# Spreading one row of a weight load unevenly over the DMA engines, reordering the last sums, and narrowing an early product to two column groups

## The chip, the cores and the metric

The kernel runs on one core of a Trainium2 chip. The metric is the device time of one execution in microseconds (us), as the median of several runs. "Span" is the shorter stretch from the first to the last instruction that the profile shows; here the time is mostly 2.0 to 2.6 us longer than the span, and over 3 us longer in three runs. A single run scatters by about 0.2 us.

## The reference

It is one decoding step of a layer, for one token: attention over a cache of 65,536 keys plus a gated feed-forward branch, on the same normalized input.

```python
xn = layernorm(x)
q = (xn @ wq)                                   # 1024 -> 32 heads of 128
scores = q . k_cache * 128**-0.5                # 4 key heads, 65,536 keys of 128
A = softmax(scores) @ v_cache  @ wo             # 4096 -> 1024
# the w1/w2 part shifts tokens; with one token only the zero padding reaches w2, so it adds 0
B = xn + gelu(layernorm(xn) @ w3) @ w4          # 1024 -> 3584 -> 1024
out = x + A + B
```

All of it is one vector times large matrices. 169.87 MB have to be read once, and nothing is reused, so the kernel streams.

## The kernel before

Loads of up to 8 MB go into three large buffers in the order wq, w3, w1 and w2, then K and V eight times, wo before the last V, and w4 last. SyncE issues every one. w4 has 3,584 rows of 2 KB, 28 for each of 128 partitions, and comes in pieces, so that TensorE can follow the landing:

```python
W4_PIECES = (8, 12, 5, 2, 1)         # rows of each partition
...
w4_v = B_w4.rearrange("(m c) n -> m c n", c=FC)          # FC = 28
c0 = 0
for n in W4_PIECES:
    go(out=t[:, c0 * D:(c0 + n) * D], in_=w4_v[:, c0:c0 + n, :].rearrange("p c n -> p (c n)"))
    c0 += n
```

The early product with wq uses four column groups of TensorE (32 output columns each). Its 64 matmuls took 4.98 us, 78 ns each in the mean, while the profile puts 479 ns to one of them:

```python
row_matmul(psq, xn_rep, lambda c, i, a: wt[:, c, 16 * i:16 * (i + 1), a, :], (512, 512))
```

The end: rows of w4 are added to the attention's projection in `psB`; the last eight rows go in halves of 256 columns into `quarters`, where the earlier sums are injected in between.

```python
with tc.issue_after(projected):
    compute_w4(early, FC - NARROW)                          # 12 wide rows, second piece
nc.vector.tensor_tensor(out=sums[:], in0=psB[0:64, :], in1=tail["o"], op=ALU.add)
narrow_rows(FC - NARROW, FC - NARROW + AHEAD, start=True)   # 5 rows, third piece
for h in range(2):
    nc.tensor.matmul(quarters[h][...], lhsT=pick[...], rhs=sums[:, 256 * h:256 * (h + 1)], ...)
narrow_rows(FC - NARROW + AHEAD, FC)                        # 2 + 1 rows
# two copies to out_t, then the store
```

## Time and profile before

| | before |
|---|---|
| time, median of 3 runs | 401.01 us (400.86 to 401.06) |
| span of the profiled run | 398.6 us |
| share of the load queue | 98.9% of 16 engines' span |
| busy: TensorE, VectorE | 57%, 53% |
| last w4 row landed (packet records) | 396.02 us |
| last four matmuls begin | 396.48 us |

The page of the profile gives averages; the packet records of the trace give the end. They do not name the DMA engine of a packet, so the sixteen engines are followed as sixteen chains of packets, by the best fit of ends, starts and sizes; the order of sizes within an engine is known from the kernel, and the prediction below says how the records follow each other. What such a fit gives for certain is the list of sixteen ends; where two engines run within a few nanoseconds of each other, it can exchange them.

### The profile page before, as it was taken

The page shows a single profiled execution, that of the slowest core. Times are in us where ns is not written, and L with a number is a line of the kernel's source. Part 1 is how long each engine was busy: PE and PEld are TensorE (multiplying, and loading weights), DVE is VectorE, ACT ScalarE, POOL GpSimd, SP SyncE. Part 2 cuts the span into 40 slices and gives each one's busy share as a digit, 9 for nine tenths or more (in the row PEclk, how much of TensorE's full clock was granted, in tenths as well). Part 3 has the DMA queues.
Part 4 walks back from the last instruction along what each step waited for, and adds up shares of the span by engine and source line. Part 5 has one row for each costly group of instructions (what it writes and reads, how often), then busy time and mean ns, then how long its engine had stood idle before and what let it go on. Part 6 is the DMA issues. An engine that isn't in the chain of part 4 may idle for free.

```text
span 398.6 us, 2575 instructions
## 1 busy us (share of the span) xinstructions
PE 225.4 (57%) x1360; PEld 44.0 (11%) x866; DVE 210.7 (53%) x160; ACT 27.1 (7%) x35; POOL 5.8 (1%) x29
## 2 busy tenths in 40 slices
PE   0251960591569238733974296519462955394986
PEld 0210000010100010011001010200020101010132
DVE  0610010974296559633963795269439942894141
ACT  1001020003000200020002000200110001002000
POOL 2000000000000000000000000000000000000000
PEclk9995996596869787966695889679956896698799
DMA  9998999999999999999999999999999998999996
GB/s 421 421 443 376 446 427 480 454 421 421 416 428 427 421 467 449 427 421 427 423 441 421 447 454 434 416 427 421 441 436 427 447 447 383 416 462 424 413 432 257
DMA packets 4144, 170.03 MB, mean 427 GB/s; under 512 B 419, under 2 KB 421, under 8 KB 678
## 3 DMA queue, kind: packets, MB, share of 16 engines
q1 hardware_dynamic: 4128, 169.87, 98.9%
q8 instruction: 9, 0.15, 0.2%
q14 instruction: 1, 0.01, 0.0%
q10 hardware_dynamic: 6, 0.00, 0.0%
HBM read 169.87 MB, written 0.00 MB: 426 GB/s over the span
## 4 chain that ended last, share of the span: by engine, by line
DMA 56%; DVE 21%; PE 17%; ACT 2%; another core or an unknown queue 2%; issue 1%; SPq 0%; DVEq 0%; ACTq 0%
DMA big<-in_A_k_cache_dram 42%; DVE big L360 15%; PE sc L365 11%; DMA big<-in_B_w_dram 8%; DMA big<-in_A_wq_dram 6%; PE oacc L415 4%; DVE p_sb L386 2%; DVE mx L370 2%; ACT p_sb L383 2%; PE psq L290 1%; SPq L187 0%; PE pm_mx L372 0%; DVE m L374 0%; PE pm_mx L379 0%
## 5 line engine op out<-in xcount | busy, mean ns | idle before, releaser
L365 PE MATMUL sc<-big,qdiag 128*128 128x512 bf16 x512 | 129.6, 414 | 66.5 <-DVE big L360 61.0
L360 DVE STREAM_TRANSPOSE big<-big 128x4096 f32<-128x4096 f32 x32 | 139.4, 4413 | 50.1 <-DMA big<-in_A_k_cache_dram 50.1
L415 PE MATMUL oacc<-big,p_sb 128*32 128x512 bf16 x512 | 43.2, 504 | 34.5 <-DVE p_sb L386 34.5
L370 DVE TENSOR_REDUCE mx<-sc 128x1 f32<-128x2048 f32 x8 | 18.3, 2292 | 29.9 <-PE sc L365 29.9
L365 PEld LDWEIGHTS <-qdiag 128*128 128x128 bf16 x128 | 13.2, 103 | 178.3 <-issue 145.7
L383 ACT ACTIVATE p_sb<-sc,nball 128x2048 bf16<-128x2048 f32 x8 | 15.7, 1968 | 220.8 <-DVE nball L381 220.8
L386 DVE STREAM_TRANSPOSE p_sb<-p_sb 128x2048 bf16<-128x2048 bf16 x8 | 18.5, 2311 | 18.0 <-ACT p_sb L383 18.0
L415 PEld LDWEIGHTS <-p_sb 128*32 128x32 bf16 x512 | 16.2, 122 | 58.2 <-DVE p_sb L386 35.1
L290 PE MATMUL psh<-big,ln_rep_b 128*32 128x512 bf16 (+1 forms) x64 | 12.4, 942 | 8.9 <-DMA big<-in_B_w_dram 8.9
L455 PE MATMUL o_acc<-big,oT 128*1 128x512 bf16 x48 | 13.2, 447 | 2.4 <-ACT p_sb L383 2.4
L372 PE MATMUL pm_mx<-ident_f,mx 128*1 128x128 f32 x8 | 2.4, 296 | 19.1 <-DVE mx L370 19.1
L424 DVE SCALAR_TENSOR_TENSOR og<-oacc,wb,og 128x512 f32<-128x512 f32 x4 | 3.0, 751 | 18.5 <-PE oacc L415 18.5
L329 DVE STREAM_TRANSPOSE h_row<-h_row 128x896 bf16<-128x896 bf16 x1 | 1.1, 1111 | 22.0 <-ACT h_row L328 22.0
L241 PE MATMUL pm_ln<-ln_rowsum_a,ones_f 128*128 128x1 f32 x2 | 0.6, 348 | 12.8 <-DVE ln_rowsum_a L239 12.8
L437 PE MATMUL pm_e<-ol,sel8big 128*128 128x129 f32 x8 | 2.3, 370 | 9.7 <-DVE ol L436 9.7
L314 POOL COPY qdiag<-qx 32x32 bf16<-32x32 bf16 x16 | 3.3, 204 | 278.7 <-PE sc L365 250.7
L290 PE MATMUL psq<-big,ln_rep_a 128*32 128x512 bf16 x64 | 5.0, 479 | 3.7 <-DMA big<-in_A_wq_dram 3.7
L232 DVE STREAM_TRANSPOSE x_t<-x_row 32x256 bf16<-32x256 bf16 x4 | 2.5, 615 | 8.4 <-DMA x_row<-in_A_x_dram 8.3
L466 DVE TENSOR_TENSOR big<-o_acc,big 1x512 f32<-1x512 f32 x2 | 1.4, 679 | 10.3 <-PE o_acc L455 10.3
L227 PE MATMUL psB<-big,hT 128*32 128x512 bf16 x40 | 4.8, 380 | 1.4 <-DMA big<-in_B_w_dram 1.3
L302 DVE CAST q_row<-psq 128x512 bf16<-128x512 f32 x1 | 0.7, 692 | 7.6 <-PE psq L290 7.6
L379 PE MATMUL pm_mx<-ident_f,rep 1*128 1x1 f32 x8 | 1.8, 229 | 5.0 <-DVE rep L376 5.0
(100 smaller groups left out, 71.9 us busy)
## 6 DMA issues: line engine op xcount, KB each, us to landing
big<-in_A_wo_dram SPq DMA_DIRECT2D x1, 8192.0 KB, 35.7
big<-in_B_w_dram SPq DMA_DIRECT2D x1, 7168.0 KB, 38.1
big<-in_B_w_dram SPq DMA_DIRECT2D x3, 2048.0 KB, 35.5
big<-in_B_w_dram SPq DMA_DIRECT2D x1, 3072.0 KB, 29.5
big<-in_B_w_dram SPq DMA_DIRECT2D x1, 1280.0 KB, 32.2
big<-in_B_w_dram SPq DMA_DIRECT2D x1, 512.0 KB
big<-in_B_w_dram SPq DMA_DIRECT2D x1, 256.0 KB, 33.1
big<-in_A_k_cache_dram SPq DMA_DIRECT2D x8, 42.2
```

Source lines behind the costliest of these rows:

```text
L227: return nc.tensor.matmul(psB[32 * j:32 * j + 32, :], lhsT=lhsT.to_broadcast([lhsT.shape[0], 32]), rhs=rhs, start=start, stop=False, tile_ ...
L232: nc.vector.transpose(out=x_t[32 * a:32 * a + 32].rearrange("p c j -> p (c j)"), in_=x_row[:, 256 * a:256 * (a + 1)].rearrange("p (i c) -> ...
L290: nc.tensor.matmul(acc[32 * q:32 * q + 32, i, 0:n], lhsT=rep[:, c, :], rhs=cols(c, i, q), start=(c == 0), stop=(c == DC - 1), tile_positio ...
L314: nc.gpsimd.tensor_copy(out=qdiag[at, LEAD:].rearrange("p (x c) -> p x c", x=4)[:, :, 32 * a:32 * a + 8], in_=qx[at, :, 8 * g:8 * g + 8])
L360: nc.vector.transpose(out=words, in_=words)
L365: nc.tensor.matmul(sc[:, e, :], lhsT=qdiag[:, c0:c0 + P], rhs=cols[:, s, e, :, b2, :, r], start=(s == 0 and b2 == 0 and r == 0), stop=(s = ...
L370: nc.vector.reduce_max(out=mx[:], in_=sc[:].rearrange("p e n -> p (e n)"), axis=AX.X)
L383: nc.scalar.activation(out=p_sb[:], in_=sc[:], func=ACTF.Exp, bias=nball[:, b:b + 1], scale=SCALE, accum_out=group["lall"][:, b:b + 1])
L386: nc.vector.transpose(out=flat, in_=flat)
L415: mm = nc.tensor.matmul(oacc[32 * q:32 * (q + 1), :], lhsT=pT[:, e, 32 * t:32 * (t + 1)], rhs=vt[:, :, e, t, :], start=(e == 0 and t < 4), ...
L424: nc.vector.scalar_tensor_tensor(out=og[:], in0=oacc[:], scalar=wb[:, 1:2], in1=og[:], op0=ALU.mult, op1=ALU.add)
L455: nc.tensor.matmul(tail["rows"][0:1, h2, :], lhsT=oT[g][:, j:j + 1], rhs=wt[:, g, j, 512 * h2:512 * (h2 + 1)], start=(g == 0 and j == 0), ...
```

## The change

It takes row 27 (the 28th) of every partition out of the common load, and loads these 128 rows by seven small transfers on 3, 3, 3, 5, 8, 8 and 8 partitions, up to four rows to a partition. The intent, as the shares show it, is to use engines that finish early. GpSimd first zeroes the columns that take these rows. The four columns so filled need their h values at the same places; a 0/1 matrix, built at the start, puts them there by four small matmuls. What `tail["o"]` holds (x and the projection of the earlier heads) is injected ahead of the second piece; of the sums in `psB`, one half is injected ahead of the third piece, and the other is added in the last copy. Six rows of the first piece run before the gather of the last heads, in place of three (this edit of the diff is not printed below). wq runs on two column groups in place of four.

No record names an engine, so the numbers 0 to 15 in this document are labels for classes of chains: 0 to 2 carry packets of all seven small loads, 3 and 4 those of the loads on 5 and on 8 partitions, 5 to 7 those on 8 alone, 8 to 15 none. In the other runs a load on k partitions is likewise labelled as using 0 to k - 1. Which engines of the chip they are is not shown.

```diff
-W4_PIECES = (8, 12, 5, 2, 1)
+W4_PIECES = (8, 11, 5, 2, 1)
+LEFT = 4
+SHARES = ((3, 0, 4), (3, 1, 4), (3, 2, 4), (5, 3, 4), (8, 32, 4), (8, 33, 4), (8, 34, 1))
+WHOLE = 27
...
+                nc.gpsimd.memset(t[:, WHOLE * D:(WHOLE + LEFT + 1) * D].bitcast(F32), 0.0)
+                for share in SHARES[:3] + W4_PIECES[:1] + SHARES[3:] + W4_PIECES[1:]:
...
+                    k, i0, m = share
+                    go(out=t[i0:i0 + 4 * k:4, WHOLE * D:(WHOLE + m) * D].rearrange("e (i n) -> e i n", i=m),
+                       in_=w4_v[m0:m0 + k * m, WHOLE, :].rearrange("(i e) n -> e i n", e=k))
...
-        row_matmul(psq, xn_rep, lambda c, i, a: wt[:, c, 16 * i:16 * (i + 1), a, :], (512, 512))
+        row_matmul(psq, xn_rep, lambda c, i, q: wt[:, c, 16 * (i % 2):16 * (i % 2 + 1), q + 2 * (i // 2), :],
+                   (512, 512, 512, 512), groups=2)
...
+def place_left():                      # h of row 27 to the partitions that hold its rows
+    for x in range(LEFT):
+        nc.tensor.matmul(pm[:, x:x + 1], lhsT=place[:, x, :], rhs=h_left[:], start=True, stop=True)
...
+    with tc.issue_after(filled):
+        filled = compute_w4(WHOLE, WHOLE + LEFT)         # the four placed columns
...
     with tc.issue_after(projected):
-        compute_w4(early, FC - NARROW)
-    nc.vector.tensor_tensor(out=sums[:], in0=psB[0:64, :], in1=tail["o"], op=ALU.add)
+        for h in range(2):
+            begun = inject(h, pick[...], tail["o"][0:64, 256 * h:256 * (h + 1)], True)
+    with tc.issue_after(begun):
+        compute_w4(early, WHOLE - NARROW)
+    nc.scalar.copy(out=sums[0][:], in_=psB[0:64, 0:256])
+    nc.vector.tensor_copy(out=sums[1][:], in_=psB[0:64, 256:512])
...
+    with tc.issue_after(inject(0, ident_f[0:64, 0:64], sums[0][:], False)):
+        narrow_rows(WHOLE - NARROW, WHOLE)
```

More of the change, by code (lines that the diff above doesn't have):

```diff
@@ L20 @@
 SLOTS = 3
-W4_PIECES = (8, 12, 5, 2, 1)
-FIRST = 3
-AT_ONCE = 1
+W4_PIECES = (8, 11, 5, 2, 1)
+LEFT = 4
+SHARES = ((3, 0, 4), (3, 1, 4), (3, 2, 4), (5, 3, 4), (8, 32, 4), (8, 33, 4), (8, 34, 1))
+WHOLE = 27
+FIRST = 6
 NARROW = 8
-AHEAD = 5
 def keep_loaded_weights(nc):
@@ L126 @@
     assert DH == P and HQ // HKV == 8 and HKV == 4 and D == 1024 and F == 3584 and S == 1
-    assert SK % UKEYS == 0 and sum(W4_PIECES) == FC
+    assert SK % UKEYS == 0 and sum(W4_PIECES) == WHOLE == FC - 1
     NB = SK // UKEYS
@@ L184, in load @@
                 w4_v = B_w4.rearrange("(m c) n -> m c n", c=FC)
-                c0 = 0
-                for n in W4_PIECES:
-                    go(out=t[:, c0 * D:(c0 + n) * D], in_=w4_v[:, c0:c0 + n, :].rearrange("p c n -> p (c n)"))
-                    c0 += n
+                nc.gpsimd.memset(t[:, WHOLE * D:(WHOLE + LEFT + 1) * D].bitcast(F32), 0.0)
+                c0, m0 = 0, 0
+                for share in SHARES[:3] + W4_PIECES[:1] + SHARES[3:] + W4_PIECES[1:]:
+                    if share in W4_PIECES:
+                        go(out=t[:, c0 * D:(c0 + share) * D], in_=w4_v[:, c0:c0 + share, :].rearrange("p c n -> p (c n)"))
+                        c0 += share
+                        continue
+                    k, i0, m = share
+                    go(out=t[i0:i0 + 4 * k:4, WHOLE * D:(WHOLE + m) * D].rearrange("e (i n) -> e i n", i=m),
+                       in_=w4_v[m0:m0 + k * m, WHOLE, :].rearrange("(i e) n -> e i n", e=k))
+                    m0 += k * m
+                assert m0 == P and c0 == WHOLE
             else:
@@ L284, with row_matmul @@
         nc.vector.tensor_copy(out=x_halves[32 * j:32 * j + 1, :], in_=x_row[0:1, 512 * j:512 * (j + 1)])
-    def row_matmul(acc, rep, cols, widths):
+    place = ogpool.tile([P, LEFT, P], BF16, name="place", tag="og")
+    nc.gpsimd.memset(place[:], 0.0)
+    m0 = 0
+    for k, i0, m in SHARES:
+        cells = place[:, 0:m, i0:i0 + 4 * k:4].rearrange("p i e -> p e i")
+        nc.gpsimd.affine_select(out=cells, in_=cells, compare_op=ALU.not_equal, fill=1.0, base=-m0,
+                                pattern=[[-1, k], [-k, m]], channel_multiplier=1)
+        m0 += k * m
+    def row_matmul(acc, rep, cols, widths, groups=4):
         for c in range(DC):
             for i, n in enumerate(widths):
-                for q in range(4):
+                for q in range(groups):
                     nc.tensor.matmul(acc[32 * q:32 * q + 32, i, 0:n], lhsT=rep[:, c, :], rhs=cols(c, i, q),
@@ L298, in compute_wq @@
         psq = ps_S.tile([P, SUBS, 512], F32, name="psq", tag="sc")
-        row_matmul(psq, xn_rep, lambda c, i, a: wt[:, c, 16 * i:16 * (i + 1), a, :], (512, 512))
+        row_matmul(psq, xn_rep, lambda c, i, q: wt[:, c, 16 * (i % 2):16 * (i % 2 + 1), q + 2 * (i // 2), :],
+                   (512, 512, 512, 512), groups=2)
         st.done("wq")
         q_row = ppool.tile([P, 2, 512], BF16, name="q_row", tag="p")
-        nc.vector.tensor_copy(out=q_row[:, 0, :], in_=psq[:, 0, :])
-        nc.scalar.copy(out=q_row[:, 1, :], in_=psq[:, 1, :])
+        nc.vector.tensor_copy(out=q_row[0:64, :, :], in_=psq[0:64, 0:2, :])
+        nc.scalar.copy(out=q_row[64:128, :, :], in_=psq[0:64, 2:4, :])
         flat = q_row[:].rearrange("p i n -> p (i n)")
@@ L316, in place_queries @@
                 in_=qx[at, :, 8 * g:8 * g + 8])
-    hT = const.tile([P, FC], BF16, name="hT")
+    hT = const.tile([P, WHOLE + LEFT], BF16, name="hT")
+    h_left = const.tile([P, 1], BF16, name="h_left")
     def compute_w3():
@@ L329, in compute_w3 @@
         nc.vector.transpose(out=h_row[:], in_=h_row[:])
-        nc.vector.tensor_copy(out=hT[:], in_=h_row[:, ::32])
+        nc.vector.tensor_copy(out=hT[:, 0:WHOLE], in_=h_row[:, 0:32 * WHOLE:32])
+        nc.vector.tensor_copy(out=h_left[:], in_=h_row[:, 32 * WHOLE:32 * WHOLE + 1])
+    def place_left():
+        pm = ps_M.tile([P, 512], F32, name="pm_h", tag="pm")
+        for x in range(LEFT):
+            nc.tensor.matmul(pm[:, x:x + 1], lhsT=place[:, x, :], rhs=h_left[:],
+                             start=True, stop=True)
+        nc.vector.tensor_copy(out=hT[:, WHOLE:], in_=pm[:, 0:LEFT])
     def compute_w12():
@@ L403, with compute_v @@
     assert NB == 2
-    def compute_v(u):
+    def compute_v(u, fill=None):
         g, b = divmod(u, NB)
@@ L425, in compute_v, with group_rows @@
                                        op0=ALU.mult, op1=ALU.add)
-        group_rows(g, og, ol)
-        return mm.ins
+        group_rows(g, og, ol, fill and (lambda: fill(mm.ins)))
     oT = {}
     tail = {}
-    def group_rows(g, og, ol):
+    def group_rows(g, og, ol, fill):
         pe = ps_M.tile([P, 512], F32, name="pm_e", tag="pm")
@@ L436, in group_rows @@
         nc.vector.tensor_reduce(out=ol[:, 0:DH], in_=og[:].rearrange("p (s d) -> p d s", d=DH), axis=AX.X, op=ALU.add)
-        tail["gathered"] = nc.tensor.matmul(pe[:, 0:DH + 1], lhsT=sel8big[:], rhs=ol[:], start=True, stop=True).ins
+        if fill is None:
+            nc.tensor.matmul(pe[:, 0:DH + 1], lhsT=sel8big[:], rhs=ol[:], start=True, stop=True)
+        else:
+            with tc.issue_after(fill()):
+                tail["gathered"] = nc.tensor.matmul(pe[:, 0:DH + 1], lhsT=sel8big[:], rhs=ol[:], start=True, stop=True).ins
         msk = small.tile([P, 16, 8], F32, name="msk", tag="msk")
@@ L460, in copy_projection @@
     def copy_projection():
-        tail["o"] = st.tiles["w4"][0:64, FC * D:FC * D + D].bitcast(F32)
-        nc.vector.tensor_scalar(out=tail["o"], in0=x_halves[:], scalar1=ln_s1[0:64, 0:1], scalar2=ln_s2[0:64, 0:1],
+        tail["o"] = st.tiles["w4"][:, (WHOLE + LEFT) * D:(WHOLE + LEFT + 1) * D].bitcast(F32)
+        nc.vector.tensor_scalar(out=tail["o"][0:64, :], in0=x_halves[:], scalar1=ln_s1[0:64, 0:1], scalar2=ln_s2[0:64, 0:1],
                                 op0=ALU.mult, op1=ALU.add)
@@ L471, in compute_w4 @@
             for j in range(2):
-                row_acc(j, hT[:, c:c + 1], wt[:, D * c + 512 * j:D * c + 512 * (j + 1)])
+                mm = row_acc(j, hT[:, c:c + 1], wt[:, D * c + 512 * j:D * c + 512 * (j + 1)])
+        return mm.ins
     compute_wq()
@@ L476 @@
     compute_w12()
+    place_left()
     for u in range(NU - 1):
@@ L484 @@
     copy_projection()
-    compute_v(NU - 1)
-    early = sum(W4_PIECES[:AT_ONCE])
-    compute_w4(0, FIRST)
-    with tc.issue_after(tail["gathered"]):
-        compute_w4(FIRST, early)
-    projected = project(HKV - 1)
-    with tc.issue_after(projected):
-        compute_w4(early, FC - NARROW)
-    sums = ogpool.tile([64, 512], F32, name="sums", tag="og")
-    nc.vector.tensor_tensor(out=sums[:], in0=psB[0:64, :], in1=tail["o"], op=ALU.add)
-    quarters = [ps_M.tile([P, 512], F32, name="pm_r", tag="pm") for _ in range(2)]
@@ L497, in quarter_acc, with first_rows @@
-    def quarter_acc(lhsT, rhs, start=False):
-        for h in range(2):
-            for j in range(2):
-                q = 2 * h + j
-                nc.tensor.matmul(quarters[h][32 * q:32 * q + 32, 0:256], lhsT=lhsT(j), rhs=rhs(j, h), start=start, stop=False,
-                                 tile_position=(0, 32 * q), skip_group_check=True)
-    def narrow_rows(lo, hi, start=False):
+    early = W4_PIECES[0]
+    def first_rows(summed):
+        with tc.issue_after(summed):
+            return compute_w4(0, FIRST)
@@ new lines @@
+    compute_v(NU - 1, first_rows)
+    with tc.issue_after(tail["gathered"]):
+        filled = compute_w4(FIRST, early)
+    with tc.issue_after(filled):
+        filled = compute_w4(WHOLE, WHOLE + LEFT)
+    with tc.issue_after(filled):
+        projected = project(HKV - 1)
+    quarters = [ps_M.tile([P, 512], F32, name="pm_r", tag="pm") for _ in range(2)]
+    sums = [ogpool.tile([64, 256], F32, name="sums_a", tag="og"), ppool.tile([64, 256], F32, name="sums_b", tag="p")]
+    pick = small.tile([64, 2, 32], F32, name="pick", tag="msk")
@@ new lines, with inject @@
+    nc.vector.tensor_copy(out=pick[:], in_=ident_f[0:64, 0:64].rearrange("p (j r) -> p j r", r=32)[:, :, 0:1].to_broadcast([64, 2, 32]))
+    def inject(h, lhsT, rows, start):
+        return nc.tensor.matmul(quarters[h][64 * h:64 * h + 64, 0:256], lhsT=lhsT, rhs=rows, start=start,
+                                stop=False, tile_position=(0, 64 * h), skip_group_check=True).ins
+    with tc.issue_after(projected):
+        for h in range(2):
+            begun = inject(h, pick[:].rearrange("p j r -> p (j r)"), tail["o"][0:64, 256 * h:256 * (h + 1)], True)
@@ L505, in narrow_rows @@
+    with tc.issue_after(begun):
+        compute_w4(early, WHOLE - NARROW)
+    nc.scalar.copy(out=sums[0][:], in_=psB[0:64, 0:256])
+    nc.vector.tensor_copy(out=sums[1][:], in_=psB[0:64, 256:512])
+    def narrow_rows(lo, hi):
         wt = st.tiles["w4"]
         for c in range(lo, hi):
-            quarter_acc(lambda j: hT[:, c:c + 1].to_broadcast([P, 32]),
-                        lambda j, h: wt[:, D * c + 512 * j + 256 * h:D * c + 512 * j + 256 * (h + 1)],
-                        start=start and c == lo)
@@ L511 @@
-    narrow_rows(FC - NARROW, FC - NARROW + AHEAD, start=True)
-    pick = small.tile([64, 2, 32], F32, name="pick", tag="msk")
-    nc.vector.tensor_copy(out=pick[:],
-                          in_=ident_f[0:64, 0:64].rearrange("p (j r) -> p j r", r=32)[:, :, 0:1].to_broadcast([64, 2, 32]))
-    for h in range(2):
-        nc.tensor.matmul(quarters[h][64 * h:64 * h + 64, 0:256], lhsT=pick[:].rearrange("p j r -> p (j r)"), rhs=sums[:, 256 * h:256 * (h + 1)], start=False,
-                         stop=False, tile_position=(0, 64 * h), skip_group_check=True)
@@ L518 @@
-    narrow_rows(FC - NARROW + AHEAD, FC)
+            for h in range(2):
+                for j in range(2):
+                    q = 2 * h + j
+                    nc.tensor.matmul(quarters[h][32 * q:32 * q + 32, 0:256], lhsT=hT[:, c:c + 1].to_broadcast([P, 32]),
+                                     rhs=wt[:, D * c + 512 * j + 256 * h:D * c + 512 * j + 256 * (h + 1)], start=False, stop=False,
+                                     tile_position=(0, 32 * q), skip_group_check=True)
+    with tc.issue_after(inject(0, ident_f[0:64, 0:64], sums[0][:], False)):
+        narrow_rows(WHOLE - NARROW, WHOLE)
@@ L520 @@
     out_t = ogpool.tile([64, 2, 256], BF16, name="out_t", tag="og")
     nc.scalar.copy(out=out_t[:, 0, :], in_=quarters[0][0:64, 0:256])
-    nc.vector.tensor_copy(out=out_t[:, 1, :], in_=quarters[1][64:128, 0:256])
+    nc.vector.tensor_tensor(out=out_t[:, 1, :], in0=quarters[1][64:128, 0:256], in1=sums[1][:], op=ALU.add)
     nc.scalar.dma_start(out=out[0, 0, :].rearrange("(j n) -> j n", j=2),
```

## The prediction

> **What bounds the kernel now.** I read the page first: busy shares, queues, chain of waits. No compute engine is above 57% of the span, while the queue that carries all loads is at 98.9%, 169.87 MB in 398.6 us.
>
> ```profile
> PE 225.4 (57%) x1360; PEld 44.0 (11%) x866; DVE 210.7 (53%) x160; ACT 27.1 (7%) x35; POOL 5.8 (1%) x29
> q1 hardware_dynamic: 4128, 169.87, 98.9%
> q8 instruction: 9, 0.15, 0.2%
> ```
>
> The reader is to see a kernel that streams: a saving counts only if the last byte lands sooner or less work follows it. Then the end of the chain of waits in order of time (start, length, what), and the timeline of the last microseconds:
>
> ```profile
> 363.32 33.11 DMA big<-in_B_w_dram
> 396.44 0.04 issue
> 396.48 0.34 PE pm_r L501 x4
> 396.82 0.02 issue
> 396.84 0.43 DVE out_t L522
> ```
> ```profile
> 391.49 2.77 PE L227 MATMUL psB<-big,hT 128*32 128x512 bf16 x24 [1.30 <-DMA big<-in_B_w_dram]
> 394.29 0.68 DVE L494 TENSOR_TENSOR sums<-psB,big 64x512 f32<-64x512 f32 x1 [5.97 <-PE psB L227]
> 395.25 0.65 PE L516 MATMUL pm_r<-sums,pick 64*64 64x256 f32 x4
> 395.83 0.40 PE L501 MATMUL pm_r<-big,hT 128*32 128x256 bf16 x8
> 396.48 0.29 PE L501 MATMUL pm_r<-big,hT 128*32 128x256 bf16 x4 [0.24 <-DMA big<-in_B_w_dram]
> ```
>
> The last w4 row lands, then 4 matmuls, two copies and the store. TensorE was ready 0.24 us before the last landing, so the landing sets the end, but with little to spare.
>
> The window of 391.5 to 396.5 us holds the opening. Columns: length, busy of PE, PEld, DVE, ACT, POOL, clock, DMA share, GB/s:
>
> ```profile
> 391.50:396.50 5.00, 4.42 (x60) 2.10 (x59) 0.68 (x1) 0.00 (x0) 0.00 (x0) 1.00 0.71 286
> ```
>
> The DMA engines are 71% busy there, not 98.9%: some are done early. The records of single DMA packets (start, duration, bytes) have no engine number, but each packet of an engine starts within some 5 ns of the end of the one before, so 16 chains can be followed. Each chain's last record is a four-byte one (the completion count). These end at 394.00, .13, .26, .44, .45, .52, .63; one at 395.27; and eight at 395.69, .71, .77, .83, .84, .91, .94 and 396.02 us from the span's start. All carry the same bytes. The eight late chains each have exactly one gap of about 1 us, at 43, 107, 158, 199, 254, 298, 339 and 385 us: beside the first eight of the nine 16,384-byte records of the instruction queue. The one at 395.27 has a short gap at 113 us beside an 8,192-byte fetch. So half of the engines are 1.1 to 2.0 us late because they also fetched instructions. The mean of the sixteen ends is 395.15, so perfect balance would be worth at most 0.87 us, 0.2% of 401.01.
>
> [...]the 26 loads of 128 partitions leave 416 four-byte records, 16 each, the one-row load of x leaves one and the two-row store two. No record names an engine. [...]nine records of 16,384 bytes. [...]here a fetch puts its engine about 1 us back for good. [...]64 matmuls of wq in 4.98 us are 78 ns each in the mean, though one lasts 479 ns.
>
> **The change, part by part.**
>
> *Moved rows.* Row 27 of all 128 partitions (8 rows of 2 KB per engine) leaves the common load, whose second piece falls from 12 to 11 rows. Its 24,576-byte packets take 914 ns, so 2 KB of one is 76 ns and eight are 0.61 us less on every engine. Back come, per engine: 0-2 get 3x4+4+4+4+1 = 25 rows, 3-4 get 13, 5-7 get 9, 8-15 none; 75+26+27 = 128. Single 2 KB packets follow each other at 80 ns in the last piece, a count record costs 9 ns. So engines 8-15: -0.61; 5-7: 0.72+0.03-0.61 = +0.14; 3-4: 1.04+0.04-0.61 = +0.47; 0-2: 2.00+0.06-0.61 = +1.45 us.
>
> *Which chain is which engine?* Here I choose. [...]its packet (6.84 to 6.93 us) fits exactly one chain's gap, and that chain ends at 394.44 or 394.45. In the first load the chains that end early started first (12.39 to 12.67 in the records' own time) and most of the late ones after (to 13.11), [...]the late eight are probably 8-15. Engine 0 is among the four first starters, with the chains ending at 394.00, .13 and .26; engines 1 and 2 are probably two of those. The 395.27 chain is probably one of 4 to 7. Then: late eight 396.02-0.61 = 395.41; the 395.27 chain at most 395.41, or 395.74 if it is engine 3 or 4; engines 1-2 395.45 to 395.71; engine 0 394.45+1.45 = 395.90. The last landing moves from 396.02 to about 395.90, by 0.12 us; up to 0.2 more if rows in groups of four run nearer 76 ns.
>
> *Issue order.* There are eight load semaphores, so the seven small loads (0.33 to 0.43 us to issue each) make SyncE wait: the order of instructions shows the last small load waiting for the semaphore of the last V, and the second w4 piece behind it. V lands at 378.81, plus 0.4 to be seen, plus two issues is 380.1, plus about 1.0 to the first packet (as for wq at the start) is 381.1 us. Until then the rings hold piece one: engines dry up at 381.7 at the earliest before, and later with the added rows. Hidden, with 0.6 us or more. A zeroing of 2,560 float columns on GpSimd (ones_f: 0.205 us for 128, some 0.1 fixed; estimate 2.2 us) also delays the issue, from 361.5 to 363.8, with V queued to 376.8. Hidden.
>
> *TensorE's tail.* Added: 8 wide matmuls for four placed columns. Two injections (0.65 us for both) move ahead of the second piece, one (about 0.3) comes after it, and one piece-two row (2 of 24 matmuls) goes. From the gather at 386.73: 12 matmuls instead of 10 (+0.25, where 0.38 us of waiting for oT was idle), projection 1.9 to about 390.55; the x sum on VectorE, now behind oT, is ready at 388.4+0.53+1.39 = 390.3; injections to 391.2. Piece two lands on engine 0 at 389.44+1.45+0.45 = 391.3. Then 22 matmuls 2.54, copy 0.4, injection 0.3, 20 narrow ones 0.73, 8 more 0.40: ready at about 395.75. The last landing, 395.90+0.46 = 396.36, still comes later. The final add in place of a copy has equal shape: I take no difference.
>
> *wq on two columns.* Sixteen fewer weight loads, but two matmuls at once instead of four: from 5 to an estimated 7 to 10 us, from 21.99 to 32 at most. The w3 load lands at 38.9 and the ring is full to 49: hidden.
>
> Sum: 0.12 to 0.3 us sooner; 401.01 becomes about 400.8 us.
>
> **Rivals.** (a) *Balance as intended*: the three low engines are the three earliest and 2 KB rows run fast; landing near 395.45, 0.55 us gained: 400.45. For it: such uneven shares look measured. Against it: the x record, which ties engine 0 to 394.44. (b) *Overloaded low engine*: the 395.27 chain is one of engines 0-2, plus 1.45 makes 396.72, 0.7 us later: 401.7. For it: the engine numbers are inferred from start order. Against it: it started eighth. (c) *A new wait takes over*: SyncE's semaphore waits leave the ring dry, or the injection ahead of piece two makes TensorE last. The arithmetic leaves 0.6 us for both; failure would cost some tenths: 401.3. (d) *Nothing moves*: engine 0 replaces the late eight almost exactly: 401.0.
>
> **Range and chances.** Most weight lies between (a) and (d); the runs before scatter by 0.2 us. 400.4 to 401.2 should hold it 8 times in 10. Two per cent is 8 us; nothing here is a tenth of that, so within 2% has 0.98.
>
> **What would show it.** Right: DMA share in the last 5 us well above 0.71; eight chains ending near 395.4; the last four matmuls still released by a w4 load, 0.1 to 0.3 sooner; wq longer with K landing unchanged. Wrong: a gap in any chain near 381; the last narrow matmuls following the ones before without a DMA wait; a lone chain past 396.

The packet at 6.84 to 6.93 us is that of the load of x; to put it, and so the chain that ends at 394.44 or 394.45, down to engine 0 was the author's estimate, as are the other engine numbers in the forecast. 394.45 + 1.45 = 395.90 in place of 396.02 is 0.12 us, and up to 0.2 more for faster rows was forecast as 0.12 to 0.3 us; but the choice of 394.45 rests on that estimate alone. The rows to a class (25, 13, 9 and none) are those of the chains in the table below. The eight load semaphores are named in the trace (101, 103 and 105 to 110), and "some 0.1 fixed" fits memsets of one column, 0.10 us each in the kernel before.

## The result, and the profile after

The changed kernel took 401.12 us (median of 6 runs, 400.68 to 401.15), the kernel before 401.03 in the same rounds (6 runs, 400.86 to 401.9). The ratio is 0.9995, with a 95% interval of 0.9982 to 1.0008: the same. Ratios here are the mean time of one kernel's fast runs over that of the other's of the same rounds, so they are not quite the ratio of the medians quoted beside them.

Means are sensitive to single runs here. Of the 31 runs of the kernel before, seven took 401.68 to 402.09 us (two of them are in these rounds); of the 34 runs of the changed kernel and of its variants with the same order of sums (all but the two four-engine kernels), none took over 401.34. Five of the seven have a span: in four it is 399.6 to 399.9 us, some 1 us longer than usual, and in one it is as usual. No trace of such a run was kept, so neither their cause nor whether the new order of sums removes them is shown.

The end of the chain of waits of the changed kernel (start, length, what):

```profile
361.86 2.25 POOLq L589
...
366.62 17.77 DMA big<-in_B_w_dram
384.38 0.02 issue
384.40 12.05 DMA big<-in_B_w_dram
396.45 0.04 issue
396.50 0.34 PE pm_r L553 x4
396.84 0.02 issue
396.86 0.42 DVE out_t L562
```

It ends as before: a w4 row lands, four matmuls, the copies. The last landing is seen at 396.45 us, against 396.44 before. GpSimd's zeroing now stands at the head of the w4 loads and took 2.25 us.

The timeline of the end:

```profile
389.56 0.65 PE L536 MATMUL pm_r<-big,pick 64*64 64x256 f32 x4
391.51 2.55 PE L236 MATMUL psB<-big,hT 128*32 128x512 bf16 x22 [1.30 <-DMA big<-in_B_w_dram]
394.10 0.36 ACT L544 COPY sums_a<-psB 64x256 f32<-64x256 f32 x1 [26.32 <-PE psB L236]
394.52 0.64 PE L536 MATMUL pm_r<-sums_a,ident_f 64*64 64x256 f32 x2 [0.46 <-ACT sums_a L544]
395.09 1.18 PE L553 MATMUL pm_r<-big,hT 128*32 128x256 bf16 x28
396.50 0.29 PE L553 MATMUL pm_r<-big,hT 128*32 128x256 bf16 x4 [0.23 <-DMA big<-in_B_w_dram]
```

The reader is to see two waits for w4: 1.30 us ahead of the second piece, 0.23 ahead of the last row. The reordering of the sums left TensorE as little ahead of the last landing as it was (0.24 before). The window of the last 5 us, in the columns that the prediction names:

```profile
391.50:396.50 5.00, 4.26 (x54) 2.06 (x53) 0.42 (x1) 0.36 (x1) 0.00 (x0) 1.00 0.74 296
```

The DMA share rose from 0.71 to 0.74 only. What the sixteen chains did is in this table. The shares differ in the number of 2 KB packets that an engine gets, so in the changed kernel a chain tells its class of engines:

| engines | rows of row 27 | end of the chain, us |
|---|---|---|
| before, all | 8 each | seven at 394.00 to 394.63, one at 395.27, eight at 395.69 to 396.02 |
| after, 0-2 | 25 | 395.57, 395.60, 395.79 |
| after, 3-4 | 13 | 394.47, 395.47 |
| after, 5-7 | 9 | 394.28, 395.62, **395.96** |
| after, 8-15 | 0 | 394.13, 394.67, and six at 395.01 to 395.63 |

So the late eight are not engines 8 to 15. Two of them are among 5 to 7, where the change adds a row, and two of 8 to 15 are early, where it takes eight away. The last landing moved by 0.05 us.

SyncE's line of the timeline shows the issue of the second piece:

```profile
379.50 0.67 SPq L194 DMA_DIRECT2D big<-in_B_w_dram  x1
380.21 4.51 SPq L190 DMA_DIRECT2D big<-in_B_w_dram  x4
```

The first line is the seventh small load, which waited 10.1 us until V, the eighth load before it, had landed (last packet at 379.03); the second begins with the second piece. Two early chains of engines 8 to 15 reached that piece at 381.77 and 382.21, and their first packet took 2.1 and 1.1 us in place of 0.84. The author reads this as the rings (the packets issued to an engine and not yet begun; in the kernel before, the large loads took 22 to 42 us from issue to landing) running short there, on engines that had time to lose; the two long packets are all that is shown of it.

Early in the kernel the product with wq took 8.87 us in place of 4.98 (139 ns to a matmul in place of 78), and the matmuls of w3 began at 39.03 in place of 38.90:

```profile
22.11 8.87 PE L307 MATMUL psq<-big,ln_rep_a 128*32 128x512 bf16 x64 [4.15 <-DMA big<-in_A_wq_dram]
...
39.03 12.43 PE L307 MATMUL psh<-big,ln_rep_b 128*32 128x512 bf16 x64 [4.05 <-DMA big<-in_B_w_dram]
```

### The profile page after: what moved, and what is told of

It reads as the page before. It is cut to its first block, busy times and chain, and to the rows that moved or that the text cites. A ratio compares the mean times of both kernels' runs of the same rounds, so it can differ in the third digit from the quotient of the medians.

```text
span 398.6 us, 2623 instructions
## 1 busy us (share of the span) xinstructions
PE 230.2 (58%) x1372; PEld 45.2 (11%) x862; DVE 211.5 (53%) x162; ACT 27.8 (7%) x36; POOL 10.0 (3%) x38
## 3 DMA queue, kind: packets, MB, share of 16 engines
q1 hardware_dynamic: 4294, 169.87, 98.9%
## 4 chain that ended last, share of the span: by engine, by line
DMA 54%; DVE 21%; PE 18%; ACT 2%; another core or an unknown queue 2%; SPq 1%; POOLq 1%; issue 1%; DVEq 0%; ACTq 0%
DMA big<-in_A_k_cache_dram 41%; DVE big L387 15%; PE sc L392 11%; DMA big<-in_B_w_dram 7%; DMA big<-in_A_wq_dram 6%; PE oacc L442 4%; DVE p_sb L413 2%; DVE mx L397 2%; PE psq L307 2%; ACT p_sb L410 2%; SPq L194 1%; POOLq L589 1%; ACT L410 0%; PE pm_mx L399 0%
## 5 line engine op out<-in xcount | busy, mean ns | idle before, releaser
L442 PE MATMUL oacc<-big,p_sb 128*32 128x512 bf16 x512 | 44.0, 520 | 34.5 <-DVE p_sb L413 34.5
L485 PE MATMUL o_acc<-big,oT 128*1 128x512 bf16 x48 | 11.9, 413 | 2.4 <-ACT p_sb L410 2.4
L307 PE MATMUL psq<-big,ln_rep_a 128*32 128x512 bf16 x64 | 8.9, 445 | 4.1 <-DMA big<-in_A_wq_dram 4.1
L320 DVE CAST q_row<-psq 64x1024 bf16<-64x1024 f32 x1 | 1.2, 1217 | 11.9 <-PE psq L307 11.9
L448 ACT COPY og<-oacc 128x512 f32<-128x512 f32 x4 | 2.3, 585 | 33.5 <-PE oacc L442 24.4
```

The costliest lines, as they stand in the source:

```text
L307: nc.tensor.matmul(acc[32 * q:32 * q + 32, i, 0:n], lhsT=rep[:, c, :], rhs=cols(c, i, q), start=(c == 0), stop=(c == DC - 1), tile_positio ...
L442: mm = nc.tensor.matmul(oacc[32 * q:32 * (q + 1), :], lhsT=pT[:, e, 32 * t:32 * (t + 1)], rhs=vt[:, :, e, t, :], start=(e == 0 and t < 4), ...
L485: nc.tensor.matmul(tail["rows"][0:1, h2, :], lhsT=oT[g][:, j:j + 1], rhs=wt[:, g, j, 512 * h2:512 * (h2 + 1)], start=(g == 0 and j == 0), ...
```

## The experiments

Eleven experiments ran, with nine new kernels; two of them are repeats. All gave correct results. Theory: the latest engine's last byte sets the end, one for one, and instruction fetches make eight engines late. Rivals: TensorE's tail sets the end; the small loads cost as much as they win; the two groups of engines have another cause.

### wq on four groups again

```diff
-        row_matmul(psq, xn_rep, lambda c, i, q: ..., (512, 512, 512, 512), groups=2)
+        row_matmul(psq, xn_rep, lambda c, i, a: wt[:, c, 16 * i:16 * (i + 1), a, :], (512, 512))
```

> The changed kernel with wq back on four column groups. Theory (wq hides behind the w3 load): its 64 matmuls go from 8.87 back to about 5.0 us, the matmuls of w3 still begin at 38.9, the time stays within 0.1 us of the changed kernel, about 401.1. Rival (the wq edit costs something later, through the first K load issued at 31.0 in place of 27.0 us, or through where the instruction fetches fall): the time falls by 0.2 us or more, or another DMA engine takes the eighth fetch and the last landing moves from 395.96.

Measured: 400.75 us (4 runs) beside 400.91 of the kernel before, ratio 0.9992 (0.9976 to 1.0008). wq took 6.03 us in this trace, not 5.0; why is not known, and the repeat below has 5.28. The last landing was at 395.92.

```profile
22.23 6.03 PE L307 MATMUL psq<-big,ln_rep_a 128*32 128x512 bf16 x64 [4.22 <-DMA big<-in_A_wq_dram]
...
39.18 12.43 PE L307 MATMUL psh<-big,ln_rep_b 128*32 128x512 bf16 x64 [7.85 <-DMA big<-in_B_w_dram]
```

The first K load was issued at 28.30 in place of 31.01, so its issue followed the wq edit. The start of w3 (39.18 against 39.03) and the issue of the first V load (51.65 against 51.50) did not. So the edit is hidden from w3 on. Since the four times were rather low, it ran again:

> The changed kernel with wq on four column groups once more, since its first four runs were the lowest of all (400.75 against 401.1 and 400.84 for the changed kernel). Theory (wq is hidden): 400.85, as the changed kernel. Rival (wq on two groups costs 0.2 us or more): 400.7 or lower again.

Measured: 400.57 us (5 runs, 400.44 to 400.91) beside 401.01 of before, ratio 0.9985 (0.9972 to 0.9997). The last landing was at 395.91, the span 398.6, both as in the changed kernel. So the trace gives no place where four groups would win, while the time is 0.15% under the kernel before; two of that kernel's nine runs are slow ones (402.09 and 401.75), and without them it is 0.09%. The changed kernel itself did not run in these rounds. The spans narrow the question: in the eleven runs of the changed kernel they are 398.4 to 398.7 us (median 398.6), in the nine with four groups 398.3 to 398.6 (median 398.5). So at most some 0.1 us can be a cost of two groups within the span. The rest of the difference lies in the time outside the span, which was 2.45 to 2.55 us in five of the first six runs of the changed kernel and 2.2 in the median of the nine.

### Row 27 by one common load

```diff
-SHARES = ((3, 0, 4), (3, 1, 4), (3, 2, 4), (5, 3, 4), (8, 32, 4), (8, 33, 4), (8, 34, 1))
+SHARES = ((P, 0, 1),)                       # and the slices without their step of 4
```

> The changed kernel with row 27 loaded by one common load of 128 partitions (8 rows on each of 16 engines) in place of the seven small ones; tail, memory zeroing and wq as changed. Theory (fetches make half the engines late; the shares took rows from engines 8-15 but gave some to late ones among 5-7): the ends spread over 2 us again, eight early ones near 394.0 to 394.7, the last near 396.0 to 396.1, so the time is within 0.1 us of the changed kernel. Rival 1 (shares worth what was intended): 0.4 us or more slower than the changed kernel. Rival 2 (the small loads cost time through issue and waits): 0.2 us or more faster.

Measured: 400.94 us beside 400.91, ratio 0.9995 (0.998 to 1.001). The chains end at 394.08 to 394.48 (seven), 395.26, and 395.69 to 396.18 (eight). The spread is back to 2 us. So what the shares win in landing is 396.18 against 395.96 in the changed kernel, 0.2 us, and that is within the scatter of the time. Rival 1, 0.4 us or more, falls; so does rival 2. This kernel keeps the new order of sums and the wq edit, so these two together moved nothing that the time resolves; no run undoes the new order alone.

### All rows on engines 0 to 3

```diff
+SHARES = ((4, 0, 4), (4, 1, 4), (4, 2, 4), (4, 3, 4), (4, 32, 4), (4, 33, 4), (4, 34, 4), (4, 35, 4))
```

> The changed kernel with all 128 rows on the four lowest engines, 32 each, in eight small loads. Theory (the latest engine's last landing sets the end one for one): engines 0-2 end at 396.15 to 396.4 (base 393.5 to 393.7 plus 32 x 0.080 plus 0.08), so the time is 0.2 to 0.5 us over the changed kernel; if the half-late engine is number 3 its end is about 397.0 and the time 1.0 us over; if it is number 4 it ends near 394.4. Rival (TensorE's tail sets the end): no change, 401.1.

Measured: 403.16 us (4 runs) beside 400.91, ratio 1.0058. The four chains with 32 rows end at 396.31, 396.37, 396.38 and 397.17: the sizes expected, with engine 3 as the half-late one, since it is in this class and in the class 3-4. But 1.2 us of landing became 2.2 us of time. The timeline shows why:

```profile
392.69 4.17 PE L236 MATMUL psB<-big,hT 128*32 128x512 bf16 x22 [1.98 <-DMA big<-in_B_w_dram]
396.89 0.36 ACT L544 COPY sums_a<-psB 64x256 f32<-64x256 f32 x1 [29.41 <-PE psB L236]
397.88 1.06 PE L553 MATMUL pm_r<-big,hT 128*32 128x256 bf16 x32
```

The 22 matmuls of the second piece take 4.17 in place of 2.55 us, and the last 32 narrow ones run through without a wait: TensorE sets the end here. The window of these 22 matmuls has a mean granted clock (the share of full speed that the trace records for TensorE, the third number from the right) of 0.60:

```profile
392.69:396.86 4.17, 4.17 (x22) 1.56 (x21) 0.00 (x0) 0.00 (x0) 0.00 (x0) 0.60 0.60 240
```

The trace's clock records drop to one half at 392.58 us, for 3.41 us; TensorE's wait of 1.98 us ended 0.1 us later. To test this, TensorE's wait was filled with eight matmuls whose result nobody reads:

```diff
+    warm = ps_O.tile([P, 512], F32, name="oacc")
+    with tc.issue_after(begun):
+        for r in range(8):
+            begun = nc.tensor.matmul(warm[0:32, :], lhsT=hT[:, 0:1].to_broadcast([P, 32]),
+                                     rhs=st.tiles["w4"][:, 0:512], start=True, stop=True, ...).ins
```

> four_engines (403.16 us, last landing 397.17, second-piece matmuls 4.17 us at a mean clock of 0.60 after 1.98 us of waiting) with 8 useless matmuls that fill TensorE's wait for the second piece. Theory (the landing cost 1.2 us and the rest, 1.0, came from the halved clock after the longer idle): the 22 matmuls take 2.55 us again, the last four are released by the last landing, and the time is about 402.2 us. Rival (the second microsecond came from something else, the small loads' issue or the tail order): 403.1 us again.

Measured: 402.39 us (4 runs) beside 400.88, ratio 1.0037. The last landing was at 397.33.

```profile
390.25 1.90 PE L545 MATMUL oacc<-big,hT 128*32 128x512 bf16 x8
392.84 2.55 PE L236 MATMUL psB<-big,hT 128*32 128x512 bf16 x22 [0.69 <-DMA big<-in_B_w_dram]
397.83 0.29 PE L558 MATMUL pm_r<-big,hT 128*32 128x256 bf16 x4 [0.24 <-DMA big<-in_B_w_dram]
```

The 22 matmuls take 2.55 us again and the last four wait for the landing again. Work without use made the kernel 0.8 us faster. So the extra microsecond of the run before was the clock, and with the clock up the landing counts one for one: 1.3 us later than before, 1.5 us longer.

### Which engine is which

Two looks, on the kernel before with w4 in pieces of 8 and 20 rows and five junk loads between them:

```diff
+for k in (4, 6, 8, 12, 14):                    # first look, 512 bytes to a partition
+    go(out=t[p0:p0 + k, 30 * D:30 * D + 256], in_=w4_v[p0:p0 + k, 0, 0:256])
+    p0 += k
```

> The kernel before with w4 in pieces of 8 and 20 rows and, between them, five junk loads of 512 bytes per partition on 4, 6, 8, 12 and 14 partitions into unused columns, to count which DMA engine is which: 5 packets on 0-3, 4 on 4-5, 3 on 6-7, 2 on 8-11, 1 on 12-13, none on 14-15. Theory (fetches go to engines 13 down to 6): the late chains are those with 3, 2 and 1 packets, the chains with none are early, the half-late one has 5 or 4. Rival (as predicted, fetches on 8-15): the chains with none are late and those with 3 are early. The time does not matter (TensorE gets its rows late, perhaps 2 us slower).

This one was inconclusive: with equal packets, chains could be assigned to classes in more than one way with the same fit. The time was 408.29 us, for TensorE gets 20 rows at once at the end. The second gave the five loads five lengths, on 6, 8, 10, 12 and 14 partitions:

> As id_engines, but the five junk loads (6, 8, 10, 12, 14 partitions) have five different row lengths (2048, 1024, 512, 4096, 1536 bytes), so that a chain of packets can't be taken for another: engines 0-5 show all five, 6-7 lack the first, 8-9 two, 10-11 three, 12-13 four, 14-15 have none. Theory (instruction fetches go to eight engines in a row from 13 down to 6): the pairs 6-7, 8-9, 10-11 and 12-13 are late with both engines and 14-15 early with both. Rival 1 (fetches on 8-15, as predicted): 14-15 late, 6-7 early. Rival 2 (no fixed set, or no row): late ones spread over several pairs. One look, time of no interest (about 408 us as with id_engines).

Measured, best fit: among 0-5 four early, one half late and one late; among 6-7, 8-9 and 14-15 one late each; among 10-11 and 12-13 both. So the theory's eight engines in a row from 13 down to 6 fall too, and so does the predicted 8 to 15. (Time 407.50 us, one run.) If the classes are the same engines in both kernels, then together with those of the changed kernel, where 3-4 hold no fully late one, the late eight are engine 5, one of 6 and 7, and six of 8 to 15.

### Engines 4 and 5 given as much as 3

```diff
+SHARES = ((3, 0, 4), (3, 1, 4), (6, 2, 4), (6, 3, 4), (6, 32, 4), (8, 33, 4))
```

> The changed kernel with the 128 rows on 3, 3, 6, 6, 6 and 8 partitions: 24 rows on engines 0-2, 16 on 3-5, 4 on 6-7. Theory (engines 4 and 5 are early, 3 half late[...], 6 and 7 late by fetches): ends 395.65 to 395.75 on engines 0-3 and 6-13, the last landing 0.2 to 0.3 us before the changed kernel's 395.96, time about 0.25 us under the changed kernel, 400.7. If 4 or 5 is a late engine after all, its end is about 396.3 and the time 0.3 us over the changed kernel. Rival (balance is worth nothing, TensorE's tail sets the end): the landing moves and the time does not.

Measured: 401.28 us (5 runs) beside 400.88, ratio 1.0007 (0.9995 to 1.002). The chains of 3-5 end at 394.89, 395.70 and 396.39, so one of 4 and 5 is late; it is 5, since the class 3-4 of the changed kernel has none that is fully late. This is the branch that was given 396.3 and 0.3 us over; it came to 396.39 and, against the unaltered changed kernel of the same rounds, 0.44 us.

> The changed kernel, unaltered, on the chip of the other runs, for a direct comparison: within 0.1 us of the kernel before, as measured first (ratio 0.9995). It also shows whether the set of late engines is the same in another execution: two of 5-7 and six of 8-15 late, the rest early, and the last landing within 0.15 us of 395.96.

Measured: 400.84 us (5 runs, 400.41 to 401.05), ratio 0.9997 (0.9985 to 1.001), last landing 395.85. Two of 5-7 and six of 8-15 are late again: as far as the classes tell, the set is the same.

### One more instruction fetch

```diff
     compute_wq()
+    extra = ps_M.tile([P, 512], F32, name="pm_x", tag="pm")
+    for r in range(140):
+        nc.tensor.matmul(extra[0:32, 0:1], lhsT=xn_rep[:, r % DC, :], rhs=xn_rep[:, 0, 0:1], start=True, stop=True)
     compute_w3()
```

> The kernel before with 140 one-column matmuls (280 TensorE instructions with their weight loads[...]) put between wq and w3, where TensorE waits for data. Theory (each 16 KiB instruction fetch puts one DMA engine about 1 us back for good): one record of the instruction queue more before the last landing, nine chains with a gap of about 1 us, and six instead of seven ends before 394.7; the last landing stays within 0.2 us of 396.02 unless the ninth fetch meets an engine that is late already, then it is near 397. Rival (the two groups have another cause, such as the engines' place): seven early and eight late ends as before. Time within 0.2 us of the kernel before in the first case of the theory.

Measured: 403.12 us (4 runs) beside 401.01, ratio 1.004 (1.0022 to 1.0057). The instruction queue has nine records before the last landing, at 36.0, 44.3, 105.9, 144.5, 195.3, 241.6, 297.1, 338.3 and 382.9 us, and the chains nine gaps of about 1 us. Still seven end before 394.6 and one at 395.41; seven of the late ones end by 396.02, and the eighth at 397.39. So the ninth fetch met an engine that was late already: by the fitted ends, eight fetches met eight different engines in every trace here, and the ninth, in the one trace that has it, met one of them again. That was the theory's second branch. It shows that a fetch is what makes an engine late: one more put the last landing back by 1.4 us, in a kernel whose loads were not touched. This is more than the gap of 1.0 to 1.1 us, because the first data packet after a gap takes 0.40 to 0.55 us longer than its like (1.41 in place of 0.91 us at 384.85 in the kernel before). The two together are some 1.5 us, and by 1.5 us the late eight of the kernel before end after the early seven in the mean. The expectation of six early ends was wrong. The rest of the 2.1 us is the clock once more: its records stand at one half for 3.41 us from 392.80.

```profile
392.88 3.96 PE L227 MATMUL psB<-big,hT 128*32 128x512 bf16 x20 [2.90 <-DMA big<-in_B_w_dram]
```

The window that holds most of them and the matmuls after them has a mean granted clock of 0.62:

```profile
393.00:397.20 4.20, 4.20 (x34) 1.75 (x33) 0.00 (x0) 0.00 (x0) 0.00 (x0) 0.62 0.50 199
```

### Rows evened out, with wq on four groups

```diff
+SHARES = ((3, 0, 4), (3, 1, 4), (5, 2, 4), (5, 3, 4), (8, 32, 4), (8, 33, 4))    # 24, 16 and 8 rows
```

> wq on four column groups and the rows on 3, 3, 5, 5, 8 and 8 partitions: 24 rows on engines 0-2, 16 on 3-4, 8 on 5-7. Theory (engine 3 half late, 5 and one of 6-7 late, 4 early): ends 395.65 to 395.75 on 0-3, 395.55 to 395.9 on the late ones of 5-7 and 395.0 to 395.7 on 8-15; last landing 0.05 to 0.15 us before the changed kernel's 395.85 to 395.96; time 400.7 to 400.8, 0.1 us under the changed kernel, at the edge of what five rounds resolve. Rival (nothing left to gain because the last landing already meets engines that only the small loads of eight partitions reach): 400.85.

Measured: 400.66 us (5 runs, 400.45 to 401.24) beside 401.01, ratio 0.9988 (0.9975 to 1.0001), last landing 395.83. It is not told apart from wq_four (400.57 in the same rounds). These two have the lowest medians here, a tenth of a per cent under the kernel before. Without that kernel's two slow runs of these rounds, the means differ by 0.05% (evened) and 0.09% (wq_four_again). That they beat it by 0.2 to 0.4 us is likely at best, and far from 2%.

### Landing and time together

| kernel | last landing in the trace | median time | difference | span of the profiled run after the landing |
|---|---|---|---|---|
| before (first runs) | 396.02 | 401.01 | 4.99 | 2.59 |
| the changed kernel | 395.96 | 401.12 | 5.16 | 2.66 |
| after_again | 395.85 | 400.84 | 4.99 | 2.65 |
| common_row | 396.18 | 400.94 | 4.76 | 2.61 |
| wq_four | 395.92 | 400.75 | 4.83 | 2.61 |
| wq_four_again | 395.91 | 400.57 | 4.66 | 2.66 |
| evened | 395.83 | 400.66 | 4.83 | 2.61 |
| balanced | 396.39 | 401.28 | 4.89 | 2.67 |
| four_warm | 397.33 | 402.39 | 5.06 | 2.62 |
| four_engines, clock halved | 397.17 | 403.16 | 5.99 | 3.62 |
| more_fetches, clock halved | 397.39 | 403.12 | 5.73 | 3.59 |

A landing is from one profiled run, a time from all runs. Where the clock stays up, the time is 4.7 to 5.2 us after the landing, and the span of the profiled run itself ends 2.59 to 2.67 us after it, over 1.5 us of landings. That is the theory's one for one, within 0.1 us in the traces; the scatter of 0.5 us in the other column is larger than what the change moves.

One rival is not separated by these runs. In all nine traces with the clock up, the last four matmuls begin 4.96 to 4.99 us after the first matmul of the second piece, so the end follows the landing of that piece as well as that of the last row. That the last landing decides rests on the wait of 0.22 to 0.24 us for a w4 load which each of the nine shows before the last four.

## Why the prediction was right or wrong

The range of 400.4 to 401.2 held the 401.12 us, and "the same" was right. The predicted gain of 0.12 to 0.3 us did not show in the time, which came out 0.09 us longer in these rounds and 0.04 shorter in after_again. Step by step:

- **Landing sets the end, with little to spare.** Right, as far as the waits show: 0.23 us of waiting before the last four matmuls, and balanced and four_warm follow the landing.
- **Half of the engines are late because they fetched instructions.** Right, and shown by more_fetches. The size was not: a fetch does not put its engine "about 1 us back" but some 1.5 us, since the packet after the gap is longer too.
- **"the late eight are probably 8-15".** This step failed. It rested on the order of first starts, where most but not all late chains came after the early ones. They are engine 5, one of 6 and 7, and six of 8 to 15. So "late eight 396.02-0.61 = 395.41" holds for six only (395.01 to 395.63); the other two got rows, and one of them ended last, at 395.96. Engine 0, predicted last at 395.90, ended with 1 and 2 at 395.57 to 395.79. The predicted last landing, 395.90, was near the measured 395.96 for a reason that was not the real one. The shares of the change, 9 rows for 5-7 and 13 for 3-4, fit engine 3 half late and 5 late rather well; evened moved the landing by no more than 0.02 to 0.13 us from the changed kernel's. That the landing came near the prediction was luck.
- **The cost of rows.** Right: the four-engine classes landed where 80 ns to a row put them.
- **Issue order "hidden, with 0.6 us or more".** The conclusion stood; the size was wrong. The small loads took 0.67 to 0.91 us to issue, not 0.33 to 0.43 (loads of 128 partitions took 0.33 to 0.53), and the two first packets of the second piece ended as if begun at 382.5 and 383.0. That is 1.8 and 2.4 us after the end of the piece's issue (380.21 plus 0.44), where the prediction had 1.0. The hope that added rows would keep the engines fed longer did not hold for engines 8 to 15, which get none. Two engines were delayed by 1.3 and 0.3 us. They were early ones, so nothing came of it. The sign that the prediction had named, a gap near 381, thus came as two long packets.
- **TensorE "ready at about 395.75".** It was ready at 396.27 (and the terms written down add up to 395.67, not 395.75). The single injection costs 0.64 us, not 0.3, and 28 narrow matmuls 1.18, not 1.13; the second piece began at 391.51, not 391.3. The reserve was 0.23 us in place of 0.6.
- **wq hidden, 7 to 10 us.** 8.87 us, and w3's start moved by 0.13 us. Whether it costs anything in time is open up to the 0.1 us above.
- **DMA share in the last 5 us "well above 0.71".** Wrong: 0.74. Of the 128 rows moved, 18 went to two late engines and 13 to the half-late one, and 16 were taken from two early ones.
- **Rival (b), overload of a low engine**, did not come about. **Rival (c)** has a sharper form than predicted. In four_engines a wait of 1.98 us ahead of the second piece cost not only itself: the clock stood at one half for 3.41 us, and the 22 matmuls took 4.17 in place of 2.55 us. In more_fetches a wait of 2.90 us was followed by the same (one half for 3.41 us, 20 matmuls in 3.96 us). Waits of 1.30 and 1.74 us in the kernel before did not: its clock was 1.00 there.

## What to carry to other kernels

When a kernel streams with its load queue as full as here (98.9%), look at the sixteen engines' ends singly: here instruction fetches left them 2 us apart (394.00 to 396.02), and the end followed the last one. Before moving bytes between engines, tag the engines with transfers of different lengths, since start order named the wrong engines here as the late ones. Near the end of such a kernel keep TensorE's waits short, or fill them: in four_engines, 0.7 us of waiting beyond the usual 1.3 came with another microsecond in clock.
